# An mLSTM cell and a gated two-layer product: moving block sums, scalings and pair stores between engines and places

## The chip, the cores and the metric

The kernel runs on one core of one Trainium2 chip. The metric is the device time of one execution in microseconds (us), the median of several executions. One execution was taken by the hardware profiler; its own time is given beside its span below. The engines are named as the profile names them: PE is TensorE's matmul, PEld its weight load, DVE is VectorE, ACT is ScalarE, POOL is GpSimd, and SP is SyncE, whose queue (SPq) issues nearly all DMAs.

## The reference

The first half is a recurrent cell over 768 time steps, for 4 batches of 8 heads with head size 40. The second half is a two-layer product with a quick GELU between the layers, on the cell's output seen as 3072 tokens of 320 numbers. All is float32.

```python
for t in range(S):                                   # S = 768; B, H, D = 4, 8, 40
    m_new  = maximum(f_gate[t] + m, i_gate[t])
    f_stab = exp(f_gate[t] + m - m_new)
    i_stab = exp(i_gate[t] - m_new)
    C = f_stab * C + i_stab * outer(v[t], k[t])      # D x D for each head
    n = f_stab * n + i_stab * k[t]
    y[t] = sigmoid(o_gate[t]) * (C @ q[t]) / maximum(abs(n @ q[t]), 1)
x = y as (3072, 320)
h = x @ w_in                                         # w_in 320 x 2048
g = h * sigmoid(1.702 * h)
out = g @ w_out                                      # w_out 2048 x 320
```

## The kernel before, in words

**Rounds.** The 768 steps are cut into six windows of 128 (`w` = 0 to 5). A window of all four batches is 512 tokens. The loop at L807 runs one round per window: the *first product* of window w (`x @ w_in`), then the *second product* of window w (`g @ w_out`). The attention of window w+1 is laid between the parts of the second product, so that TensorE stays fed. Within each engine, instructions run in program order; the order is written out by hand and nothing is scheduled automatically.

**First product.** In round 0 it is done plainly (`up`, L545). In rounds 1 to 5 it is a Strassen-like scheme with seven products (`up_fast`, L608), in eight passes `j` = 0 to 7 of 256 hidden units each. A pass makes a tile `g` (128 partitions, 2 x 512): DVE adds parts at L658, L659 and L662, ACT copies at L655 and L666, GpSimd adds at L667 (for j below 6; DVE does it at L669 for the last two), and ACT applies GELU at L606 (`gelu_fast` of pass j-1 runs in pass j). In round 1, passes 0 to 3 also hold `weight_sums` (L687), one GpSimd operation of 128x1280 each. While a next window remains, DVE transposes its q and k in passes 1 to 6 (L353).

**Second product.** In round 0, `down` (L671) makes 16 blocks. In rounds 1 to 5, `down_fast` (L714) makes 14 blocks, seven for each pair `c` of batches (c = 0, 1); a block is one product of 16 TensorE matmul records, whose result DVE adds to an output tile (L730, L732). The scheme needs sums of hidden blocks. `a00`, `a10` and `a11` are `hidden(w, j, 0)`, `hidden(w, j, 1)` and `hidden(w, j + 4, 1)`, each 128x512. `hidden_sums` (L695) forms, for j = 0 to 3: s1 = a10 + a11 (L705), s2 = s1 - a00 (L706), and last, in place, a10 = a00 - a10 (L703). GpSimd does j = 0 and 1, after passes 6 and 7 of the first product (L845); DVE does j = 2 and 3 after the last pass (L849). `last_sums` (L708, DVE, L712) later turns s2 into a fourth sum. Block 2 reads s2, block 3 reads the changed a10, block 4 reads s1, block 6 reads the fourth sum.

**Attention of the next window.** `attention(w)` (L796) gives a table `at` of block numbers; after block i of the second product, all calls with that number run. For rounds 1 to 4 the numbers are 0, 0, 1, 3, 1, 4, 5, 6, 10, 12; for round 0 (argument w = 1) they are 0, 1, 3, 3, 5, 6, 8, 9, 13, 14. The calls are, in order:

- after block 0: `columns` (L320, ACT makes exponentials: L329 and then L333), `decay` for both pairs (L511, GpSimd, L516: state times a column that L333 made), and then `scale` for both pairs (L519, GpSimd, L523: v times a column that L329 made, giving `vw`).
- `weights` (L365, ACT L381 and GpSimd L385), `open_gates` (L335, ACT).
- `carry` (L525): TensorE multiplies k by `vw` into `p_c` (L533); DVE adds that to the decayed state (L542), with its own decay (L516, DVE) in between.
- `scores` (L388, TensorE L405, DVE L408), then `values` for each pair (L432): TensorE L449 and L457, DVE L463 and L464, then `outputs` (L410), which ends with two DVE operations at L424 that write the pair's rows `y`, one batch each.
- `seam_out` (L488): stores `y` to DRAM, two DMAs per batch (`x_row`, `x_rest`), called inside `outputs` after each batch. All are issued by SP.
- `seam_in` (L498): three SP loads bring the rows back in another layout (`q_sq<-x_row`, `q_sq<-x_rest` twice). `seam_turn` (L506): DVE transposes them into `xT` (L508), the input of the next first product.

In round 0, `input_sums` (L580, DVE L584 to L587, four operations of 128x512 per call) runs after blocks 11 and 12. `token_sums` (L589, DVE L595 to L600) opens each fast first product, and its sums feed the fifth product of pass 0.

Of the kernel before, what the change touches and what calls it, by code (L numbers as in the profile page):

```python
# [8 lines left out]
FP = mybir.dt.float32  # L9
# [3 lines left out]
OP = mybir.AluOpType  # L13
# [4 lines left out]
L = 128  # L18
# [8 lines left out]
def kernel(  # L27
# [12 lines left out]
    nc = tc.nc  # L40
# [22 lines left out]
    sp = ctx.enter_context(tc.tile_pool(name="sp", bufs=4))  # L63
    op = ctx.enter_context(tc.tile_pool(name="op", bufs=2))
    rows = ctx.enter_context(tc.tile_pool(name="rows", bufs=2, space=bass.MemoryType.DRAM))
# [4 lines left out]
    V, A, G, T = nc.vector, nc.scalar, nc.gpsimd, nc.tensor  # L70
# [38 lines left out]
    def load(w, what, bs=slice(0, B)):  # L109
        hs = slice(bs.start * H, bs.stop * H)  # L110
        for c in what:
            if c == "o" and w not in eo:
                eo[w] = ld.tile([L, BH, D], FP, tag="eo", bufs=1, name="eo")
            dst, src = {"k": (k_of(w), k), "q": (q_st, q), "v": (v_st, v), "o": (eo.get(w), o_gate)}[c]
            if w and c in "kv":
                for i, t, r in ((0, slice(0, L), slice(0, L)), (1, slice(0, HL), slice(HL, L)),
                                (1, slice(HL, L), slice(0, HL))):
                    x = src[:, :, w * L + t.start:w * L + t.stop, :].rearrange("b (p two) s d -> two s (b p) d", two=2)
                    nc.sync.dma_start(out=dst[r, i::2, 0:D], in_=x[i])  # L119
                continue  # L120
            nc.sync.dma_start(out=dst[:, hs, 0:D],
                              in_=src[bs, :, w * L:(w + 1) * L, :].rearrange("b h s d -> s (b h) d"))
# [97 lines left out]
    kT, qT, ys, xT, gs, o_ps, sums, vw, x_row = {}, {}, {}, {}, {}, {}, {}, {}, {}  # L220
# [189 lines left out]
    def outputs(w, hs, u):  # L410

        n = hs.stop - hs.start
        c, b = divmod(hs.start // H, 2)
        den = work.tile([L, n, 1], FP, tag="den", name="den")
        V.tensor_scalar(out=den, in0=u[:, :, D:D1], scalar1=-1.0, scalar2=1.0, op0=OP.mult, op1=OP.max)
        V.tensor_tensor(out=den, in0=u[:, :, D:D1], in1=den, op=OP.max)
        V.reciprocal(out=den, in_=den)
        z = eo[w][:, hs, :]
        V.scalar_tensor_tensor(out=z, in0=z, scalar=1.0, in1=u[:, :, 0:D], op0=OP.add, op1=OP.mult)
        if b == 0:  # L420
            ys[w, c] = work.tile([L, 2, DM + 64], FP, tag="y", name="y")
        for x in range(n // H):
            y, h = ys[w, c][:, b + x], slice(hs.start + x * H, hs.start + x * H + H)
            V.scalar_tensor_tensor(out=y[:, 0:DM].rearrange("p (h d) -> p h d", d=D), in0=eo[w][:, h, :], scalar=0.5,  # L424
                                   in1=den[:, x * H:(x + 1) * H].to_broadcast([L, H, D]), op0=OP.mult, op1=OP.mult)
            if w:
                seam_out(w, c, x)
        if w == 0:
            y = ys[w, c][:, b:b + n // H]
            G.tensor_copy(out=y[:, :, DM:DM + 64], in_=y[:, :, DM - 64:DM])  # L430
# [54 lines left out]
        at, m = (c * 768, 64) if n == 0 else (c * 768 + 512, 32)  # L485
        return q_sq[:, at:at + 8 * m].rearrange("r (b y) -> r b y", y=m)

    def seam_out(w, c, b):  # L488

        if b == 0:  # L490
            x_row[w, c] = (rows.tile([2, 4, L, 64], FP, name="x_row"), rows.tile([2, 2, L, 32], FP, name="x_rest"))
        y = ys[w, c][:, b, :]
        for x, at, m in ((x_row[w, c][0], 0, 64), (x_row[w, c][1], 256, 32)):
            g = x.shape[1]
            nc.sync.dma_start(out=x[b].rearrange("g t y -> t g y"),
                              in_=y[:, at:at + g * m].rearrange("t (g y) -> t g y", y=m))

    def seam_in(w, c):  # L498
        for n, gs_ in ((0, (0,)), (1, (0, 64))):
# [187 lines left out]
    def weight_sums(n):  # L687
        out, a, b = ((t1, w01, w00), (t2, w11, t1), (w01, w11, w01), (t4, w10, t2))[n]
        G.tensor_tensor(out=out, in0=a, in1=b, op=OP.subtract)

    def hidden(w, j, b):

        return gs[w, j].rearrange("p i (c two t) -> p i c two t", two=2, t=L)[:, :, :, b, :]

    def hidden_sums(w, j, late):  # L695
        if j % 2 == 0 and not late:
            for x in (1, 2):
                sums[w, x, j // 2] = sp.tile([128, 2, 2, 2, L], FP, tag="g", name="s")
        s1, s2 = (sums[w, x, j // 2][:, j % 2] for x in (1, 2))
        a00, a10, a11 = hidden(w, j, 0), hidden(w, j, 1), hidden(w, j + 4, 1)  # L700
        engine = G if j < 2 else V
        if late:
            engine.tensor_tensor(out=a10, in0=a00, in1=a10, op=OP.subtract)  # L703
        else:
            engine.tensor_tensor(out=s1, in0=a10, in1=a11, op=OP.add)  # L705
            engine.tensor_tensor(out=s2, in0=s1, in1=a00, op=OP.subtract)  # L706

    def last_sums(w, c, js):  # L708

# [38 lines left out]
    def run(calls):  # L748
        for f, *args in calls:
            f(*args)  # L750
# [39 lines left out]
    def weights_in(n):  # L790
        for p in beside[n][0]:
            convert(p)
        for p in beside[n][1]:
            fetch(p)

    def attention(w):  # L796
        at = (0, 1, 3, 3, 5, 6, 8, 9, 13, 14) if w == 1 else (0, 0, 1, 3, 1, 4, 5, 6, 10, 12)
        calls = [[(columns, w), (decay, w, 0, 0), (decay, w, 1, 0), (scale, w, 0), (scale, w, 1)],
                 [(weights, w, 0)], [(weights, w, 1)], [(carry, w, 0), (carry, w, 1)], [(open_gates, w)],
                 [(scores, w, 0), (scores, w, 1)], [(values, w, 0), (seam_in, w, 0)], [(values, w, 1), (seam_in, w, 1)],  # L800
                 [(seam_turn, w, 0)], [(seam_turn, w, 1)]]
        side = {}
        for i, c in zip(at, calls):
            side.setdefault(i, []).extend(c)
        return side

    for w in range(NW):  # L807
        more = w + 1 < NW
        if w == 0:
            for j in range(NF // 2):  # L810
                if j % 2 == 0:
                    weights_in(j // 2)
                    up(w, j)
                if j == 0:
                    load(1, "o")
                if j < B:
                    (carry if j % 2 else scale)(0, j // 2)
                if j == 3:
                    masks()
                    gates(1)  # L820
                if j == 4:
                    load(1, "v")
                    columns_in(1)
                    spread(1)
                if j >= B:
                    transposes(1, j - B)
        else:
            token_sums(w)
            if more:
                gates(w + 1)  # L830
                load(w + 1, "o")
            for j in range(NF // 2):
                up_fast(w, j)
                if w == 1 and j < 4:
                    weight_sums(j)
                if more and j == 2:
                    load(w + 1, "vk")
                    columns_in(w + 1)
                    spread(w + 1)
                if more and j:  # L840
                    for n in ((), (0, 2), (4,), (6, 1), (3,), (5, 7), ())[j - 1]:
                        block_transposes(w + 1, n)
                if more and j == 7:
                    columns_turn(w + 1)
                if j in (6, 7):  # L845
                    for late in (False, True):
                        hidden_sums(w, j - 6, late)
            gelu_fast(w, NF // 2 - 1)
            run([(hidden_sums, w, j, late) for late in (False, True) for j in (2, 3)])  # L849
        side = attention(w + 1) if more else {}  # L850
        if w == 0:
            columns_turn(1)

            blocks = [(lambda b=b, n=n: down(w, b, n)) for n0 in (0, 2) for b in range(B) for n in (n0, n0 + 1)]
        else:
            blocks = down_fast(w, 0) + down_fast(w, 1)
        for i, block in enumerate(blocks):
            if w == 0 and i < 6:
                weights_in(4 + i)
            if w + 2 < NW and i == (6 if w == 0 else 0):  # L860
                load_gates(w + 2)
            if w + 2 < NW and i == 13:
                load_squares(w + 2, "kq" if w else "k")
            if w == 0 and i == 15:
                load_squares(w + 2, "q")
            block()
            run(side.get(i, []))
            if w == 0 and i in (11, 12):
                input_sums(slice(0, 4) if i == 11 else slice(4, 8))


# [28 lines left out]
```

## Time and profile before

| what | value |
|---|---|
| times of three runs | 490.03, 488.68, 487.78 us; median 488.68 us |
| the profiled execution | 487.78 us, of which its span is 486.1 us |
| granted TensorE clock, mean | 0.998 |
| PE busy | 471.6 us (97%), 4926 instructions |
| DVE busy | 348.3 us (72%) |
| ACT busy | 189.7 us (39%) |
| POOL busy | 149.3 us (31%), 135 instructions |
| chain that ended last, by engine | PE 62%, POOL 10%, SPq 8%, DVE 6%, DMA 6% |
| POOL L705, L706, L703: one 128x512 operation | 1278, 1274, 1273 ns, ten of each |
| DVE L705, L706, L703: the same shapes | 670, 692, 901 ns, ten of each |
| POOL L516 (decay), L523 (scale) | 1155 ns, ten; 1398 ns, twelve |

A line of a timeline or group gives the start and the length in us, the engine, the code line, the operation, the tiles (written `out<-in`), their shapes and the count `xN` of instructions merged into the line. In square brackets stands how long the engine was idle before it and what ended that idleness. A list of waits reads: engine, tile and line that waited, `<-` what it waited for, then the total in us, how many times, and the longest. Matmuls are pipelined and the profile models their ends, so a line of TensorE may overlap the next one; distances between starts are the safer measure.

### The profile page before, as it was taken

To read this page: it belongs to the slowest core of one execution; us is meant where nothing else is said; L and a number is where in the kernel's file an instruction comes from. 1 tells how busy PE (TensorE), PEld (TensorE's weight loads), DVE (VectorE), ACT (ScalarE), POOL (GpSimd) and SP (SyncE) were. 2 spreads that over 40 slices of the span, in tenths; PEclk is the share of its full clock that TensorE was granted. 3 is DMA by queue.
4 is the path that set the end of the run, shared out by engine and by line. 5 is a ranking of instruction groups with operands and counts; after the bars stand their busy time and mean duration, and the time that the engine had idled before them with its cause. 6 is when DMAs were issued, how large, how long until landed. Compare 5 with 4: busy or idle time off the path is not lost.

```text
span 486.1 us, 12090 instructions
## 1 busy us (share of the span) xinstructions
PE 471.6 (97%) x4926; PEld 378.4 (78%) x4926; DVE 348.3 (72%) x691; ACT 189.7 (39%) x429; POOL 149.3 (31%) x135
## 2 busy tenths in 40 slices
PE   8999999999999999999999999999999999999995
PEld 5774446777668889767889877899877899877995
DVE  5675977988778975868985868985868965644711
ACT  4746558700453900354900254710254720254100
POOL 6020003400398700127620136630036630136100
PEclk9999999999999999999999999999999999999999
DMA  8999988005997014989304899604899504200000
GB/s 182 174 310 145 271 134 192 3 13 131 207 169 137 2 42 109 160 150 131 69 21 101 168 154 125 92 18 102 165 167 119 88 18 102 61 1 0 1 27 29
DMA packets 157352, 52.19 MB, mean 107 GB/s; under 512 B 127056, under 2 KB 154736, under 8 KB 157296
## 3 DMA queue, kind: packets, MB, share of 16 engines
q1 hardware_dynamic: 157296, 51.42, 56.9%
q8 instruction: 39, 0.64, 0.6%
q14 instruction: 17, 0.14, 0.1%
HBM read 43.86 MB, written 7.54 MB: 106 GB/s over the span
## 4 chain that ended last, share of the span: by engine, by line
PE 62%; POOL 10%; SPq 8%; DVE 6%; DMA 6%; issue 5%; ACT 2%; DVEq 0%; POOLq 0%
PE p_out L727 25%; PE p_h L625 15%; PE p_h L630 5%; PE p_h L555 4%; DMA wt<-m_row 3%; SPq L363 3%; PE p_o L449 2%; POOL vw L523 2%; SPq L119 2%; PE p_i L457 2%; POOL g L667 2%; SPq L311 2%; PE p_s L405 2%; PE p_out L676 1%; PE p_c L533 1%
## 5 line engine op out<-in xcount | busy, mean ns | idle before, releaser
L667 POOL TENSOR_TENSOR g<-g,parts 128x512 f32<-128x512 f32 x30 | 38.3, 1276 | 213.1 <-DVE parts L659 202.0
L655 ACT COPY parts<-p_h 128x256 f32<-128x256 f32 x40 | 15.0, 374 | 160.3 <-PE p_h L625 157.6
L727 PE MATMUL p_out<-w_out_sb,g 128*128 128x160 f32 x480 | 69.6, 301 | 0.1
L727 PEld LDWEIGHTS p_out<-w_out_sb,g 128*128 128x128 f32 x480 | 66.6, 190 | 1.1 <-issue 0.2
L625 PE MATMUL p_h<-xT,w_in_sb 128*128 128x256 f32 x240 | 66.9, 388 | 0.0
L606 ACT ACTIVATE g<-g 128x512 f32<-128x512 f32 x80 | 50.0, 631 | 36.2 <-DVE g L662 25.1
L625 PEld LDWEIGHTS p_h<-xT,w_in_sb 128*128 128x128 f32 x240 | 43.7, 190 | 20.2 <-issue 8.3
L732 DVE TENSOR_TENSOR o_sb<-o_sb,p_out 128x160 f32<-128x160 f32 x70 | 20.5, 315 | 41.5 <-PE p_out L727 20.8
L727 PE MATMUL p_out<-t_sb,s 128*128 128x160 f32 x320 | 47.1, 300 | 0.0
L658 DVE TENSOR_TENSOR t_x<-p_h,parts 128x256 f32<-128x256 f32 x40 | 16.7, 418 | 39.1 <-PE p_h L630 34.6
L727 PEld LDWEIGHTS p_out<-t_sb,s 128*128 128x128 f32 x320 | 44.4, 190 | 0.2
L625 PE MATMUL p_h<-t_x,s_in 128*128 128x256 f32 x160 | 41.1, 379 | 0.9 <-DVE t_x L595 0.9
L630 PE MATMUL p_h<-xT,w_in_x 64*128 64x512 f32 x160 | 39.7, 615 | 0.0
L381 ACT ACTIVATE wt<-wt,cols 128x64 f32<-128x64 f32 x160 | 38.8, 333 | 0.1
L676 PE MATMUL p_out<-w_out_sb,g 128*128 128x320 f32 x128 | 36.0, 436 | 0.7 <-DVE w_out_sb L234 0.7
L625 PEld LDWEIGHTS p_h<-t_x,s_in 128*128 128x128 f32 x160 | 30.3, 190 | 5.4 <-issue 1.3
L676 PEld LDWEIGHTS p_out<-w_out_sb,g 128*128 128x128 f32 x128 | 23.8, 190 | 10.6 <-DVE w_out_sb L234 1.2
L659 DVE TENSOR_TENSOR parts<-p_h,t_x 128x512 f32<-128x512 f32 x40 | 27.7, 692 | 3.5
L666 ACT COPY g<-p_h 128x512 f32<-128x512 f32 x30 | 17.4, 580 | 31.9 <-PE p_h L630 26.5
L555 PE MATMUL p_h<-xT,w_in_sb 128*128 128x512 f32 x64 | 29.5, 604 | 0.1
L516 POOL TENSOR_TENSOR state_mid<-state,cols 128x328 f32<-128x328 f32 x10 | 11.4, 1155 | 59.4 <-ACT cols L333 55.6
L662 DVE TENSOR_TENSOR g<-p_h,parts 128x512 f32<-128x512 f32 x40 | 27.7, 691 | 1.4
(185 smaller groups left out, 850.3 us busy)
## 6 DMA issues: line engine op xcount, KB each, us to landing
wt<-m_row SPq DMA_DIRECT2D x40, 128.0 KB, 3.7
k_sq<-in_k_dram SPq DMA_DIRECT2D x16, 320.0 KB, 6.2
q_sq<-in_q_dram SPq DMA_DIRECT2D x16, 320.0 KB, 10.1
out_dram<-o_sb SPq DMA_DIRECT2D x24, 160.0 KB
eo<-in_o_gate_dram SPq DMA_DIRECT2D x5, 640.0 KB, 8.9
bits<-in_moe_w_in_dram SPq DMA_DIRECT2D x6, 512.0 KB
x_row<-y SPq DMA_DIRECT2D x20, 128.0 KB, 2.4
q_sq<-x_row SPq DMA_DIRECT2D x10, 256.0 KB, 2.6
```

The costliest lines, as they stand in the source:

```text
L381: A.activation(out=x[:, h, :], in_=x[:, h, :], func=AF.Exp, scale=-1.0, bias=cols[w][:, c * PH + h:c * PH + h + 1])
L555: T.matmul(ph[j][i], w_in_sb[:, c, f * 128:(f + 1) * 128], x[:, c, :], start=(first and c == 0), stop=(not first and c == 1))
L606: A.activation(out=gs[w, j][:, i, :], in_=gs[w, j][:, i, :], func=AF.Gelu_apprx_sigmoid)
L625: T.matmul(out, a, x[n], start=start, stop=stop)
L630: T.matmul(row, w_in_x[r, j, :], rest_x[r, 2, :], start=not late, stop=late)
L659: V.tensor_tensor(out=y[:, half_w:3 * half_w].rearrange("p (a t) -> p a t", a=2), in0=flat[:, half_w:3 * half_w].rearrange("p (a t) -> p a ...
L662: V.tensor_tensor(out=g[:, 1, :], in0=row1, in1=y[:, half_w:3 * half_w], op=OP.add)
L666: A.copy(out=g[:, 0, :], in_=row0)
L667: G.tensor_tensor(out=g0, in0=g0, in1=u, op=OP.add)
L676: T.matmul(po, gs[w, f // 2][:, f % 2, b * L:(b + 1) * L], w_out_sb[:, f, :], start=(f == 0), stop=(f == NF - 1))
L727: T.matmul(po, a(f), b[:, f, :], start=(f == 0), stop=(f == NH - 1))
L732: V.tensor_tensor(out=dst, in0=x, in1=po, op=OP.add)
```

## The change

Four things change.

1. `hidden_sums` is split. `hidden_difference` does a10 = a00 - a10 first, for all four j, on GpSimd, after passes 2 to 5 of the first product, when the GELU of tile j is long done. The other sums are built on that difference d: s2 = a11 - d and then s1 = s2 + a00. GpSimd does them for j = 0, 1 after passes 6 and 7, DVE for j = 2, 3 after the last pass, with both s2 ahead of both s1.
2. In `attention`, the two `scale` calls stand ahead of the two `decay` calls.
3. `seam_out` is a call of its own for a whole pair instead of a call per batch inside `outputs`. It issues both batches' `x_row` stores and then both `x_rest` stores. For pair 1 ScalarE issues them instead of SP. In rounds 1 to 4, pair 0's stores and loads follow block 6 instead of block 5.
4. In round 0, `seam_turn` of pair 0 follows block 12 instead of 13, and the second `input_sums` follows block 13 instead of 12.

```diff
     def outputs(w, hs, u):
...
-            if w:
-                seam_out(w, c, x)
...
-    def seam_out(w, c, b):
+    def seam_out(w, c):
...
-            nc.sync.dma_start(out=x[b].rearrange("g t y -> t g y"),
-                              in_=y[:, at:at + g * m].rearrange("t (g y) -> t g y", y=m))
+            for b in range(2):
+                (nc.scalar if c else nc.sync).dma_start(
+                    out=x[b].rearrange("g t y -> t g y"),
+                    in_=ys[w, c][:, b, at:at + g * m].rearrange("t (g y) -> t g y", y=m))
...
-    def hidden_sums(w, j, late):
...
-        engine = G if j < 2 else V
-        if late:
-            engine.tensor_tensor(out=a10, in0=a00, in1=a10, op=OP.subtract)
-        else:
-            engine.tensor_tensor(out=s1, in0=a10, in1=a11, op=OP.add)
-            engine.tensor_tensor(out=s2, in0=s1, in1=a00, op=OP.subtract)
+    def hidden_difference(w, j):
+
+        a00, a10 = hidden(w, j, 0), hidden(w, j, 1)
+        G.tensor_tensor(out=a10, in0=a00, in1=a10, op=OP.subtract)
+
+    def hidden_sums(w, js, engine):
+        for j in js:
...
+            d, a11 = hidden(w, j, 1), hidden(w, j + 4, 1)
+            engine.tensor_tensor(out=sums[w, 2, j // 2][:, j % 2], in0=a11, in1=d, op=OP.subtract)
+        for j in js:
+            s1, s2 = (sums[w, x, j // 2][:, j % 2] for x in (1, 2))
+            engine.tensor_tensor(out=s1, in0=s2, in1=hidden(w, j, 0), op=OP.add)
...
-        at = (0, 1, 3, 3, 5, 6, 8, 9, 13, 14) if w == 1 else (0, 0, 1, 3, 1, 4, 5, 6, 10, 12)
-        calls = [[(columns, w), (decay, w, 0, 0), (decay, w, 1, 0), (scale, w, 0), (scale, w, 1)],
+        at = (0, 1, 3, 3, 5, 6, 8, 8, 9, 12, 14) if w == 1 else (0, 0, 1, 3, 1, 4, 5, 6, 6, 10, 12)
+        calls = [[(columns, w), (scale, w, 0), (scale, w, 1), (decay, w, 0, 0), (decay, w, 1, 0)],
...
-                 [(scores, w, 0), (scores, w, 1)], [(values, w, 0), (seam_in, w, 0)], [(values, w, 1), (seam_in, w, 1)],
-                 [(seam_turn, w, 0)], [(seam_turn, w, 1)]]
+                 [(scores, w, 0), (scores, w, 1)], [(values, w, 0)], [(seam_out, w, 0), (seam_in, w, 0)],
+                 [(values, w, 1), (seam_out, w, 1), (seam_in, w, 1)], [(seam_turn, w, 0)], [(seam_turn, w, 1)]]
...
-                if j in (6, 7):
-                    for late in (False, True):
-                        hidden_sums(w, j - 6, late)
+                if 2 <= j < 6:
+                    hidden_difference(w, j - 2)
+                if j >= 6:
+                    hidden_sums(w, (j - 6,), G)
             gelu_fast(w, NF // 2 - 1)
-            run([(hidden_sums, w, j, late) for late in (False, True) for j in (2, 3)])
+            hidden_sums(w, (2, 3), V)
...
-            if w == 0 and i in (11, 12):
+            if w == 0 and i in (11, 13):
                 input_sums(slice(0, 4) if i == 11 else slice(4, 8))
```

More of the change, by code (lines that the diff above doesn't have):

```diff
@@ L486, in x_square @@
         return q_sq[:, at:at + 8 * m].rearrange("r (b y) -> r b y", y=m)
-    def seam_out(w, c, b):
-        if b == 0:
-            x_row[w, c] = (rows.tile([2, 4, L, 64], FP, name="x_row"), rows.tile([2, 2, L, 32], FP, name="x_rest"))
-        y = ys[w, c][:, b, :]
+    def seam_out(w, c):
+        x_row[w, c] = (rows.tile([2, 4, L, 64], FP, name="x_row"), rows.tile([2, 2, L, 32], FP, name="x_rest"))
         for x, at, m in ((x_row[w, c][0], 0, 64), (x_row[w, c][1], 256, 32)):
             g = x.shape[1]
-            nc.sync.dma_start(out=x[b].rearrange("g t y -> t g y"),
-                              in_=y[:, at:at + g * m].rearrange("t (g y) -> t g y", y=m))
+            for b in range(2):
+                (nc.scalar if c else nc.sync).dma_start(
+                    out=x[b].rearrange("g t y -> t g y"),
+                    in_=ys[w, c][:, b, at:at + g * m].rearrange("t (g y) -> t g y", y=m))
     def seam_in(w, c):
@@ L693, in hidden @@
         return gs[w, j].rearrange("p i (c two t) -> p i c two t", two=2, t=L)[:, :, :, b, :]
-    def hidden_sums(w, j, late):
[L696 to L700, printed above, removed]
-        engine = G if j < 2 else V
-        if late:
-            engine.tensor_tensor(out=a10, in0=a00, in1=a10, op=OP.subtract)
-        else:
-            engine.tensor_tensor(out=s1, in0=a10, in1=a11, op=OP.add)
-            engine.tensor_tensor(out=s2, in0=s1, in1=a00, op=OP.subtract)
+    def hidden_difference(w, j):
[3 more added lines that the diff above has]
+        for j in js:
+            if j % 2 == 0:
+                for x in (1, 2):
+                    sums[w, x, j // 2] = sp.tile([128, 2, 2, 2, L], FP, tag="g", name="s")
+            d, a11 = hidden(w, j, 1), hidden(w, j + 4, 1)
[3 more added lines that the diff above has]
+            engine.tensor_tensor(out=s1, in0=s2, in1=hidden(w, j, 0), op=OP.add)
     def last_sums(w, c, js):
```

## The prediction, made blind

> **What bounds the kernel now.** I read the busy times first, then the list of waits, then TensorE's timeline round by round, and last the timelines of whoever it waits for. TensorE is busy 97% of the 486.1 us span, so only its idle time can go.
>
> ```profile
> PE 471.6 (97%) x4926; PEld 378.4 (78%) x4926; DVE 348.3 (72%) x691; ACT 189.7 (39%) x429; POOL 149.3 (31%) x135
> ```
>
> ```profile
> PE p_c L533 <- POOL vw L523: 3.5, 8, 0.6
> PE p_i L457 <- issue: 1.7, 2, 1.0
> ...
> PE p_h L625 <- DVE t_x L595: 0.9, 1, 0.9
> ```
>
> Three kinds matter: eight waits of the carry for scaled values, one at the start of round 1, and two in which it waited for nothing visible. The first kind, in round 2, on TensorE, on GpSimd and on ScalarE:
>
> ```profile
> 236.06 2.34 PE L727 MATMUL p_out<-w_out_sb,g 128*128 128x160 f32 x16
> 238.97 1.14 PE L533 MATMUL p_c<-vw,k_st 64*64 64x41 f32 x64 [0.57 <-POOL vw L523]
> 240.40 1.14 PE L533 MATMUL p_c<-vw,k_st 64*64 64x41 f32 x64 [0.28 <-POOL vw L523]
> 241.47 2.44 PE L727 MATMUL p_out<-t_sb,s 128*128 128x160 f32 x16
> 243.84 2.10 PE L405 MATMUL p_s<-qT,kT 40*64 40x64 f32 x128
> ```
>
> ```profile
> 235.25 2.42 POOL L516 TENSOR_TENSOR state_mid<-state,cols 128x328 f32<-128x328 f32 x2 [3.74 <-ACT cols L333]
> 237.63 2.71 POOL L523 TENSOR_TENSOR vw<-v_st,cols 128x656 f32<-128x656 f32 x2
> ```
>
> ```profile
> 234.50 0.26 ACT L329 ACTIVATE cols<-cols 128x64 f32<-128x64 f32 x1
> 234.66 0.51 ACT L333 ACTIVATE cols<-raw 64x32 f32<-64x32 f32 x2
> ```
>
> GpSimd, idle until 235.25, does two decays first, and TensorE waits for each scaling in turn. The start of round 1, on TensorE and on DVE:
>
> ```profile
> 120.86 1.03 PE L625 MATMUL p_h<-xT,w_in_sb 128*128 128x256 f32 x4
> ...
> 123.42 1.10 PE L625 MATMUL p_h<-t_x,s_in 128*128 128x256 f32 x4 [0.90 <-DVE t_x L595]
> ...
> 127.44 0.70 PE L625 MATMUL p_h<-xT,w_in_sb 128*128 128x256 f32 x2
> ```
>
> ```profile
> 121.06 0.71 DVE L508 STREAM_TRANSPOSE xT<-q_sq 128x512 f32<-128x512 f32 x1 [1.72 <-DMA q_sq<-x_row]
> ```
>
> Here pair 1's rows come back late, so L508 is late, so the sums of L595 are late.
>
> **What the Trainium skill says.** "Perfetto Trace Analysis" (Identifying the Most-Contended Engine) warns that matmul busy time is no good measure of headroom. The trace agrees in small: the carry's second wait shows 0.28 us idle, but 0.43 is lost by distances of starts. So I measure stalls by starts. "SBUF — State Buffer" (Who interferes with whom) says that a DVE instruction with two SBUF inputs contends with a GpSimd one that reads SBUF, and one with at most one SBUF input, outside the 2-port modes, doesn't. The trace agrees: a pair of L712 (two SBUF inputs) takes 0.75 us with GpSimd idle (457.19) and 2.76 beside the scalings (237.87); a transpose L353 takes 1.14 beside a GpSimd addition (219.34), 1.10 without (220.30). "DMA: Bandwidth & Descriptors" (Issuing engines are not separate DMA queues) says that a second issuing engine saves only the sequencer's time. Here just that is late: in round 0 SP issued pair 1's first store at 113.73, though DVE had finished both rows at 112.0 (L424, 111.12 + 0.89).
>
> **Part 1, scalings ahead of decays.** From a product to small matmuls the starts lie 243.84 - 241.47 = 2.37 apart. Unhindered, the carry would start at 236.06 + 2.37 = 238.43; it starts at 238.97, 0.54 late. One carry takes 1.0 (in round 0 both took 2.01 with no wait, 85.86 to 87.87), so the second would start at 239.97, but does at 240.40, 0.43 late. Rounds 1, 3 and 4 give 0.54 to 0.55 for the first (164.63 for 164.09, 313.20 for 312.66, 386.61 for 386.06) and about the same second. Sum 4 x 0.97 = 3.9 us. Afterwards a scaling waits for L329 alone, which ends at 234.76: at 1.36 us each the scalings end at 236.1 and 237.5, at the trace's longest (1.73) at 236.5 and 238.2. TensorE needs them at 238.43 and 239.43, so all 3.9 goes with 1.2 to spare. The decays now run from 237.5 to 239.9 (1.18 each); queued behind them are the four masks L385, which began at 240.30 before, so nothing there is later. DVE's L542 wants decay and carry, and the carry itself ends only at 239.4. Next late at the carry would be k_st, issued by 223.9 and landing some 6.0 us later, at 230: no danger. Round 0's carry did not wait, so nothing is won there.
>
> **Part 2, the sums.** DVE loses two L703 a round (1.83 us at 235.25). GpSimd gains two operations, 2 x 1.27, and all four differences move into passes 2 to 5, where it idles 2.0 to 3.6 us ahead of each L667 in rounds 2 to 5. They fit, and the sums behind them, four operations instead of six, end near 230.2 instead of 231.5. DVE, with both s2 first, has them by 234.0; block 2 needs the third at 233.89 + 1.09 = 234.98. Block 3 loses a wait that did not stall. Value zero, hidden by TensorE's own products. But DVE must now keep up with a TensorE 1 us earlier: L408 of pair 0 ended 247.5 and was needed at 248.24. The 1.83 us saved covers that; without it 0.3 us a round would come back.
> Round 1 is the tight place, as weight_sums fill GpSimd there:
>
> ```profile
> 141.84 1.28 POOL L667 TENSOR_TENSOR g<-g,parts 128x512 f32<-128x512 f32 x1
> 143.06 2.92 POOL L689 TENSOR_TENSOR t_sb<-w_out_sb,t_sb 128x1280 f32<-128x1280 f32 x1
> 145.94 1.28 POOL L667 TENSOR_TENSOR g<-g,parts 128x512 f32<-128x512 f32 x1
> 148.43 1.28 POOL L667 TENSOR_TENSOR g<-g,parts 128x512 f32<-128x512 f32 x1 [1.21 <-ACT g L666]
> ```
>
> Three differences push pass 4's L667 to end near 149.65 (from 147.2). ScalarE's GELU waits for it, and queued behind that is the copy L666 of pass 5, then done at about 150.8 (from 148.4). TensorE rewrites that buffer in pass 7 at 150.96. Cost 0, at most 0.4 us.
>
> **Part 3, stores and transposes.** Round 0: ScalarE, idle from 94.7 to 121.5, issues pair 1's four stores from 112.05, some 0.45 us each by SP's rows; nothing waits behind them. The second x_row goes out near 112.5 instead of 114.82, so SP's loads start about 2.3 us earlier than 118.23, though still after pair 0's (until 113.05). The last rows land by about 120, not 121.9; L508 runs by 120.7, DVE copies the last block by 121.4, and L595 ends near 121.85. TensorE wants it at 122.2. Pass 0 took 127.44 - 120.86 = 6.58 us against 276.00 - 270.97 = 5.03 in round 3: 1.55 lost, of which I take 1.5; if the loads land 1 us later than I think, 0.6.
> Rounds 1 to 4: pair 0's stores wait behind block 6's output store (ready 0.4 us after them, issue 0.6), about 1 us later, but its loads were issued by 260.45 for a transpose at 266.14. SP no longer holds block 6's store from 254.7 to 260.54, so DVE's wait for an output buffer (4.74 us at 264.77) goes. Both off the path: zero.
> The two issue waits (0.96 at 181.20, 0.78 at 255.47) fall just after SP's x_row stores; moving those may end them or not. Between a gain of 1.8 and a loss of 1.0 (as much again in a round spared so far), I take zero.
>
> **Sum.** 3.9 + 1.5 = 5.4 us. The profiled execution took 487.78, 1.7 more than its span; it would take 482.4. The median of the three runs lies 0.9 above that execution, so I forecast 483.3.
>
> **Rivals.**
> *A, the issue waits go too:* 483.3 - 1.8 = 481.5. For it: both followed the stores by half a microsecond. Against: rounds 3 and 4 issued the same stores at the same place without one.
> *B, only the scalings pay:* the loads of round 0 still arrive after 121.5, because their 2.4 to 3.3 us to landing don't shrink. 488.7 - 3.9 = 484.8.
> *C, the carry doesn't move as said:* something I can't see, a buffer of p_c or a later scaling, is late next; only round 1's start pays, 488.7 - 1.5 = 487.2. Against it: every other input of the carry is 1 us early or more.
> *D, slower:* the differences block DVE in passes 2 to 5. Two passes of round 3 hold 1.38 us of DVE idle time (at 291.68), so it decides from 0.69 us per difference; at a full 1.27 each, two passes lose 2 x 1.27 - 1.38 = 1.16. Twice in each of four rounds: 9.3 us. 488.7 + 9.3 - 5.4 = 492.6. Against it: the L353 pair of the SBUF rule above, and DVE's additions there read PSUM and keep 0.69 us beside L667.
>
> **How the numbers follow.** Forecast 0.52 (own range 482.0 to 484.6: parts 1 and 3 within their bounds), A 0.16, B 0.14, C 0.11, D 0.07. The measurement can tell about 0.5% from no change, 2.4 us. Faster by more holds forecast, A and B: 0.82; within it C, 0.11; slower D, 0.07. The range from 481.0 to 487.0 takes in A and B, and leaves out most of C, and D.
>
> **What would show it.** Right: no p_c wait on vw, starts 2.37 and 1.0 apart at the carry; rounds 2 to 4 about 1 us shorter each; L508 of pair 1 before 121, no wait on L595; L703 inside passes 2 to 5 on GpSimd with L353 still 1.1. Wrong: a TensorE wait on ACT in pass 7 of round 1, L353 or L659 longer, or a new wait at p_o or p_s for L408 or L542.

## The result and the profile after

The changed kernel took 481.97 us (median of six runs, 481.72 to 483.82), against 489.36 us (six runs, 487.78 to 491.04) for the kernel before, measured beside it. The ratio is 0.9854, with a 95% interval from 0.9824 to 0.9885. The forecast was 483.3, the range 481.0 to 487.0. The time is right; the experiments show that a good part of the reason is not.

The profiled execution is the longest of the six, 483.82 us with a span of 481.8. TensorE's granted clock was 0.73 in the mean there between 178.9 and 185.3 us, and 32 matmuls of round 1 (starts from 179.14 to 185.27) took 6.13 us instead of the 4.46 that they take in other rounds (398.12 to 402.58); these 1.67 us are not the change's. The other five executions have spans of 479.5 to 480.0.

The busy times, from the page after:

```profile
PE 471.4 (98%) x4926; PEld 379.7 (79%) x4926; DVE 336.8 (70%) x681; ACT 189.4 (39%) x429; POOL 158.0 (33%) x145
```

TensorE works as long as before in a shorter span. GpSimd has ten operations and 8.7 us more, DVE ten operations and 11.5 us fewer. TensorE's waits after (total, times, longest):

```profile
PE p_i L455 <- issue: 2.1, 2, 1.3
PE p_idle L189 <- DVE one L197: 1.1, 1, 1.1
PE p_out L674 <- DVE w_out_sb L234: 0.7, 1, 0.7
PE p_s L394 <- DVE wt L396: 0.5, 1, 0.5
PE p_t L345 <- DMA q_sq<-in_q_dram: 0.4, 1, 0.4
...
```

The eight waits of the carry for `vw` and the wait for `t_x` are gone; the two in which it waited for nothing visible have stayed. The 0.4 us for a load of q stand at 6.0 us, ahead of all that was changed, and had no like in the list of before. Round 2's carry, on TensorE and then on GpSimd (start, duration):

```profile
235.44 2.34 PE L728 MATMUL p_out<-w_out_sb,g 128*128 128x160 f32 x16
237.71 2.08 PE L531 MATMUL p_c<-vw,k_st 64*64 64x41 f32 x128
239.72 2.44 PE L728 MATMUL p_out<-t_sb,s 128*128 128x160 f32 x16
```

```profile
234.21 2.75 POOL L521 TENSOR_TENSOR vw<-v_st,cols 128x656 f32<-128x656 f32 x2 [4.56 <-ACT cols L329]
236.92 1.79 POOL L514 TENSOR_TENSOR state_mid<-state,cols 128x328 f32<-128x328 f32 x2
```

Product, both pairs' carry and next product start 2.27 and 2.01 us apart. They were 2.91 and 2.50 before, so 0.64 and 0.49, together 1.13 us a round, are saved. The start of round 1, on DVE:

```profile
119.56 1.03 DVE L506 STREAM_TRANSPOSE xT<-q_sq 128x512 f32<-128x512 f32 x2
120.93 0.49 DVE L678 COPY o_sb<-p_out 128x320 f32<-128x320 f32 x1 [0.34 <-PE p_out L674]
121.34 0.42 DVE L593 TENSOR_TENSOR t_x<-xT 128x256 f32<-128x256 f32 x1
```

Pair 1's transposes no longer wait for a DMA and end before 121. Pass 0 takes 5.19 us (120.73 to 125.92) instead of 6.58.

Where the time went, by the starts of the first products: rounds 2, 3 and 4 take 73.10, 72.17 and 72.04 us; they took 74.20, 73.42 and 73.17, so 1.10, 1.25 and 1.13 are saved. Round 1 takes 75.40 instead of 75.91. Without the 1.67 of the clock it saves 2.18: 1.39 in pass 0, 1.14 at the carry, less 0.32 by which its wait for nothing visible is longer. The rest is unchanged: from the start of the last second product to the end of DVE's last operation it was 30.95 and is 30.95 us.

So far all looks as predicted. What the changed kernel can't show is which part paid.

### The profile page after: what moved, and what is told of

Read it like the earlier page. It is cut to its first block, busy times and chain, and to the rows that moved or that the text cites. A ratio compares the mean times of both kernels' runs of the same rounds, so it can differ in the third digit from the quotient of the medians.

```text
span 481.8 us, 12086 instructions
## 1 busy us (share of the span) xinstructions
PE 471.4 (98%) x4926; PEld 379.7 (79%) x4926; DVE 336.8 (70%) x681; ACT 189.4 (39%) x429; POOL 158.0 (33%) x145
## 4 chain that ended last, share of the span: by engine, by line
PE 91%; DVE 3%; SPq 2%; POOL 1%; issue 1%; DMA 1%; ACT 0%; POOLq 0%; DVEq 0%
PE p_out L728 33%; PE p_h L623 26%; PE p_h L628 8%; PE p_out L674 7%; PE p_h L553 5%; PE p_c L531 3%; PE p_o L447 2%; PE p_s L405 2%; PE p_i L455 2%; PE p_h L559 1%; PE p_o L437 1%; DMA wt<-m_row 1%; SPq L363 1%; PE p_t L345 1%; SPq L119 0%
## 5 line engine op out<-in xcount | busy, mean ns | idle before, releaser
L728 PE MATMUL p_out<-w_out_sb,g 128*128 128x160 f32 x480 | 71.3, 306 | 0.0
L728 PEld LDWEIGHTS p_out<-w_out_sb,g 128*128 128x128 f32 x480 | 68.2, 194 | 1.1
L733 DVE TENSOR_TENSOR o_sb<-o_sb,p_out 128x160 f32<-128x160 f32 x70 | 21.5, 319 | 45.8 <-PE p_out L728 45.4
L521 POOL TENSOR_TENSOR vw<-v_st,cols 128x656 f32<-128x656 f32 x12 | 16.6, 1402 | 59.8 <-ACT cols L329 59.8
L674 PEld LDWEIGHTS p_out<-w_out_sb,g 128*128 128x128 f32 x128 | 23.8, 190 | 10.6 <-DVE w_out_sb L234 1.2
L657 DVE TENSOR_TENSOR parts<-p_h,t_x 128x512 f32<-128x512 f32 x40 | 27.7, 692 | 3.5
```

The source lines that it names most:

```text
L657: V.tensor_tensor(out=y[:, half_w:3 * half_w].rearrange("p (a t) -> p a t", a=2), in0=flat[:, half_w:3 * half_w].rearrange("p (a t) -> p a ...
L674: T.matmul(po, gs[w, f // 2][:, f % 2, b * L:(b + 1) * L], w_out_sb[:, f, :], start=(f == 0), stop=(f == NF - 1))
L728: T.matmul(po, a(f), b[:, f, :], start=(f == 0), stop=(f == NH - 1))
L733: V.tensor_tensor(out=dst, in0=x, in1=po, op=OP.add)
```

## The experiments

The theory on trial first was the prediction's own: part 1 (scalings first) is worth 3.9 us, part 3 (stores) 1.5, part 2 (sums) nothing. The rival, that only the parts together do it, had no mechanism yet. All times are medians; ratios are to the kernel before, measured beside each.

### One part at a time

**Scalings first alone**, on the kernel before:

```diff
-        calls = [[(columns, w), (decay, w, 0, 0), (decay, w, 1, 0), (scale, w, 0), (scale, w, 1)],
+        calls = [[(columns, w), (scale, w, 0), (scale, w, 1), (decay, w, 0, 0), (decay, w, 1, 0)],
```

> The kernel before with one edit: the two scalings stand ahead of the two decays. Theory (the carry's stall on the scaled values is the main part): 2.7 to 3.9 us faster than before, no wait of L533 on vw in rounds 1 to 4; if DVE, still with its L703, cannot follow, up to 0.3 us a round shows up as a new TensorE wait at p_o or p_s. Rival (the saved DVE time of the moved sums is what pays): within 1 us of before.

Measured: 488.99 against 488.19 us, ratio 1.0013 (1.0 to 1.0026). No gain at all. The carry's wait is gone, but another has its place. Its list of waits, then DVE and GpSimd in round 2:

```profile
PE p_out L727 <- DVE g L703: 3.5, 4, 0.9
```

```profile
234.64 3.47 DVE L703 TENSOR_TENSOR g<-g 128x512 f32<-128x512 f32 x2
```

```profile
234.22 3.34 POOL L523 TENSOR_TENSOR vw<-v_st,cols 128x656 f32<-128x656 f32 x2 [3.34 <-ACT cols L329]
```

DVE's two differences take 3.47 us instead of 1.83, since GpSimd now runs the scalings beside them, and block 3, which reads them, waits 0.88 us per round. The scalings are held up too: 3.34 instead of 2.71. By starts the carry of round 2 takes 2.00 us instead of 2.50, and block 3 ahead of it 3.46 instead of 2.91.

**Sums alone**, on the kernel before (`hidden_difference` and the new `hidden_sums`, as in the diff of the change):

> The kernel before with only the block sums moved and rebuilt (four differences on GpSimd in passes 2 to 5). Theory: within 0.5 us of before, the stall of the carry unchanged at 0.5 to 0.6 us on its first matmul, L353 still 1.1 us in passes 2 to 5. Rival (the sums pay): 2 us or more faster. Rival (GpSimd blocks DVE): slower, L353 above 1.5 us.

Measured: 484.55 us, ratio 0.9919 (0.9905 to 0.9934), about 4 us faster by the ratio. The part priced at zero is the largest. GpSimd in its round 2:

```profile
233.89 1.43 POOL L516 TENSOR_TENSOR state_mid<-state,cols 128x328 f32<-128x328 f32 x2 [4.96 <-DMA wt<-m_row]
235.28 2.90 POOL L523 TENSOR_TENSOR vw<-v_st,cols 128x656 f32<-128x656 f32 x2
```

The decays still come first, but a pair takes 1.43 us, not 2.42: DVE ended its sums at 233.83 and is out of the way. From block 3 to the carry and on it is 2.27 and 2.33 us (starts at 234.70, 236.97, 239.30), against 2.91 and 2.50 before. Of the 1.13 lost per round 0.33 is left, with the order untouched; the 0.80 won is 3.2 us in four rounds.

**Stores alone**, on the kernel before (`seam_out`, the table `at` and the place of the input sums):

> The kernel before with only the stores, their places, ScalarE as issuer for pair 1, and round 0's transposes and input sums moved. Theory: 1.5 us faster than before, all of it at the start of round 1 (pass 0 there 5.0 us instead of 6.6), the carry's stall in rounds 1 to 4 as before. Rival (stores matter in every round): 3 us or more.

Measured: 487.19 us, ratio 0.9978 (0.9965 to 0.999), about 1 us faster. `t_x` is not waited for, and the carry's wait is as before:

```profile
PE p_c L531 <- POOL vw L521: 3.5, 8, 0.6
PE p_i L455 <- issue: 2.3, 2, 1.3
```

**Everything but the scalings**, the changed kernel with the decays first again:

> The changed kernel with the decays ahead of the scalings again. Theory: 3.9 us slower than the changed kernel, about 1.5 to 2 us faster than before; L533 waits on vw eight times again. Rival (the sums pay): within 1 us of the changed kernel.

Measured: 482.53 us, ratio 0.989 (0.9866 to 0.9915), 0.56 more than the changed kernel and not 3.9. Its carry in round 2:

```profile
235.74 2.41 PE L531 MATMUL p_c<-vw,k_st 64*64 64x41 f32 x128
238.07 2.44 PE L728 MATMUL p_out<-t_sb,s 128*128 128x160 f32 x16
```

2.33 us from start to start, where the changed kernel has 2.01: again 0.33 lost per round, 1.3 in four rounds. The times bound it loosely: 0.56 between the medians, 1.8 between the ratios. (In the profiled executions the waits for nothing visible are 0.6 us in all here and 2.1 in the changed kernel; they may cover part of the stall in the medians.)

So the theory had fallen. The new one: **the decays were slow because DVE ran beside them**. Two operations that each take two values from SBUF, one on DVE and one on GpSimd, hold each other up. Before, the decays and DVE's differences L703 both began at 235.25. DVE's line of then, and the shortest, middle and longest time (ns) of one decay (the shortest is of round 0, where no L703 runs):

```profile
235.25 1.83 DVE L703 TENSOR_TENSOR g<-g 128x512 f32<-128x512 f32 x2
```

```profile
L516 POOL TENSOR_TENSOR state_mid<-state,cols x10: 736/1182/1283, 80.2 to 384.1; 128x328 f32<-128x328 f32 x10
```

The sums cure this by taking two operations off DVE; the order on GpSimd alone only chooses which pair of operations meets.

### The contention by itself

**Only the two differences of DVE left out**, on the kernel before:

```diff
-            run([(hidden_sums, w, j, late) for late in (False, True) for j in (2, 3)])
+            run([(hidden_sums, w, j, False) for j in (2, 3)])
```

> The kernel before, in which DVE leaves out the two differences L703 of hidden blocks 2 and 3 that it did last (block 3 of each second product then multiplies values that half lack their difference); everything else, the decays first too, is as before. Theory (the decays were slow because they ran beside these two operations on DVE; each took 1.2 us instead of 0.7): the pair of decays takes 1.43 instead of 2.42 us, the scalings come 1.0 earlier, the carry loses 0.33 a round instead of 0.97, and the time falls by 2.6 us or more, to 485.6 or less; as far as 484.5 if all of what the sums alone won comes from this. Rival 1 (the gain of the sums alone came from the new form, in which s2 is ready first, or from GpSimd's free time): no gain, 488.2. Rival 2 (it came from issue waits that happened to shrink from 1.7 to 0.9): 488.2, with a shorter stall at the carry and longer issue waits.

Measured: 483.99 us, ratio 0.991 (0.9891 to 0.9929). GpSimd and TensorE in round 2:

```profile
233.89 1.43 POOL L516 TENSOR_TENSOR state_mid<-state,cols 128x328 f32<-128x328 f32 x2 [3.77 <-ACT cols L333]
```

```profile
236.97 2.41 PE L533 MATMUL p_c<-vw,k_st 64*64 64x41 f32 x128
239.31 2.44 PE L727 MATMUL p_out<-t_sb,s 128*128 128x160 f32 x16
```

The old form of the sums, the old order and no work more for GpSimd: the same 1.43, the same 2.34, and as much gain as the sums alone. The new form of the sums (rival 1) is not needed for it. Issue waits (rival 2) are 0.9 us here and 1.7 before: 0.8 of the 4.4 us between the medians, while the carry's 0.80 a round makes 3.2.

**Two additions put back on DVE**, on the changed kernel with the decays first (482.53):

```diff
             hidden_sums(w, (2, 3), V)
+            spare = work.tile([128, 2, 2, L], FP, tag="y", name="spare")
+            for j in (2, 3):
+                V.tensor_tensor(out=spare, in0=hidden(w, j, 0), in1=hidden(w, j + 4, 1), op=OP.add)
```

> The kernel after with the decays first again (the run of that name took 482.53), and on DVE, behind the four sums of hidden blocks 2 and 3, two additions more of two values in SBUF (128x512, 0.65 us each), whose result nobody reads. They fall beside GpSimd's decays and scalings. Theory (DVE and GpSimd hold each other up): decays and scalings together take 1.2 to 1.3 us longer than 4.3, the carry's wait for vw comes back at 1.0 to 1.5 us a round in four rounds, and the time is 4 to 6 us longer, 486.5 to 488.5. Rival (only DVE's own lateness counts): decays and scalings keep 1.43 and 2.9, no wait for vw, and as much longer as the same kernel with the transposition: 0 to 1 us.

**One transposition instead of them:**

```diff
             hidden_sums(w, (2, 3), V)
+            spare = work.tile([128, 512], FP, tag="y", name="spare")
+            for j in (3,):
+                V.transpose(out=spare, in_=gs[w, j].rearrange("p a b -> p (a b)")[:, 0:512])
```

> As the kernel with the two extra additions, but with one transposition on DVE instead of them (128x512, one value in SBUF, 1.1 us), whose result nobody reads. Theory (only operations with two values in SBUF hold GpSimd up): decays and scalings keep 1.43 and 2.9 us a pair, no new wait at the carry, and 482.5 to 483.5. Rival (any work of DVE beside GpSimd holds it up, or DVE's lateness itself costs): the decays and scalings take 1 us longer, 485 to 487.

Measured: with the additions 485.64 us, ratio 0.9946 (0.9929 to 0.9963); with the transposition 482.40, ratio 0.9875 (0.9856 to 0.9895), no more than without. In the kernel with the additions, DVE, GpSimd and TensorE's wait:

```profile
234.09 1.83 DVE L854 TENSOR_TENSOR spare<-g 128x512 f32<-128x512 f32 x2
```

```profile
234.24 2.27 POOL L514 TENSOR_TENSOR state_mid<-state,cols 128x328 f32<-128x328 f32 x2 [4.97 <-DMA wt<-m_row]
```

```profile
PE p_c L531 <- POOL vw L521: 3.0, 8, 0.6
```

In the kernel with the transposition, DVE and GpSimd:

```profile
232.25 0.70 DVE L854 STREAM_TRANSPOSE spare<-g 128x512 f32<-128x512 f32 x1
```

```profile
232.40 1.43 POOL L514 TENSOR_TENSOR state_mid<-state,cols 128x328 f32<-128x328 f32 x2 [4.96 <-DMA wt<-m_row]
```

Two additions bring back all three signs of before: 1.83 on DVE, 2.27 instead of 1.43 on GpSimd, eight waits of the carry. The transposition leaves the decays at 1.43. Its list has three short waits of the carry for `vw`, 0.5 us in all, which were not expected; by starts the carry loses 0.03 us a round more than without it. DVE's copies and additions of a product from TensorE (L731, L733, 0.32 us each), which have at most one value in SBUF, lie beside these decays too. Two reservations: the transposition took 0.70 us, not the 1.1 expected, so it met the first decay for 0.55 us only; and the additions cost 3.1 us, less than the 4 to 6 expected. The scalings behind them took 2.71 us, no longer than without them (2.90), and by starts the carry lost 1.00 us a round instead of 0.33.

**Scalings first and stores, without the sums:**

> The kernel after with the sums of before: scalings ahead of decays and the new stores, without the third difference on GpSimd. The prediction's own steps give 483.3 for it (the sums were worth nothing). The theory that the sums carry the gain: the scalings run beside DVE's L703, block 3 waits for L703 some 0.9 us a round as in the scalings alone, and only the 1.0 us of the stores is left: 487 to 488.5.

Measured: 487.35 us, ratio 0.9974 (0.9961 to 0.9986), what the stores alone give. Its list of waits:

```profile
PE p_out L725 <- DVE g L701: 3.5, 4, 0.9
```

The prediction's steps give 483.3 for this kernel. They are 4 us off.

### What ScalarE's issuing is worth

```diff
-                (nc.scalar if c else nc.sync).dma_start(
+                nc.sync.dma_start(
```

> The kernel after with one edit: SP, not ScalarE, issues the stores of pair 1 too. It tells what ScalarE's issuing is worth beside the later place of the stores. Theory (the 1.4 us at the start of round 1 come from ScalarE's earlier issue): SP issues pair 1's stores behind pair 0's loads again, L506 of pair 1 is late, TensorE waits for L593 at the start of round 1 some 0.9 us, and the time is 1.0 to 1.5 us longer than after, 483 to 483.5. Rival (the regrouping of the stores does it): 482.

Measured: 482.51 us, ratio 0.9863 (0.9839 to 0.9887), 0.54 more than the changed kernel and half of what was expected. The intervals of the two kernels overlap, so the trace has to decide. TensorE's wait at the start of round 1:

```profile
PE p_h L623 <- DVE t_x L593: 0.5, 1, 0.5
```

0.47 us instead of 0.90 before. SP issues both `x_row` stores back to back now, from 112.97, so the load of these rows goes out at 115.90 instead of 118.23 and the large transposition runs at 119.54; only the rows of `x_rest`, loaded at 118.17, are late. About half of the wait goes by ScalarE's issuing. The other half goes by the grouping, or by the moved transposes and input sums of round 0, which were not tried alone.

### The waits for nothing visible

In TensorE's timelines of both kernels and of all nine experiments so far these two waits stand at the same place: behind 56 or 57 of the 64 matmul records of pair 1's `p_i` in round 1 and behind 62 or 63 in round 2 (a record or so can be missing), whatever the stores do. Only their length differs, 0.25 to 1.3 us. The kernel with the sums alone has a third one, which the expectations below overlook: 0.57 us in round 3, behind the fourth record of the product after `p_i`. In its list of waits:

```profile
PE p_out L730 <- issue: 0.6, 1, 0.6
```

Counted in TensorE's matmul records, it comes 886 behind the one of round 2, as that comes 886 behind the one of round 1. In the changed kernel the one of round 2 began at 252.9, before its `x_row` stores were issued at 253.55. So three kernels moved the place: idle matmuls at the start, `keep_busy`, were put as fewer or more instructions with about the same streaming time.

```diff
-    keep_busy(8)
+    keep_busy_f(2)
...
-    keep_busy(4)
+    keep_busy_f(1)
```

`keep_busy_f` is the same in fp32, 512 columns each.

> The kernel after with 9 matmuls fewer on TensorE before round 0's products: twelve idle bf16 ones are put as three fp32 ones of half the width of output, with the same streaming time. It shifts the place of every later instruction in TensorE's program by 9 matmuls and changes nothing else. The two waits for nothing visible (2.1 us, at the 57th matmul of 64 of p_i in round 1 and at the last in round 2; the same two places in every kernel so far, whatever the stores do) are open. Theory (they belong to a place in the instruction stream): both move by 9 matmuls and so out of p_i into the products behind it; in rounds 3 and 4, where no wait is seen, the same count already puts the place there. Then up to 2 us less than after: 480 to 481.5. Rival 1 (they belong to transfers or to p_i itself): same two places in p_i, 482. Rival 2: they follow the count but stay as long or longer in the products: 482 to 483.

```diff
-    keep_busy(8)
+    for _ in range(17):
+        T.matmul(p_idle[:, 0:240], idle, idle[:, 0:120].unsqueeze(1).to_broadcast([128, 2, 120]), start=True, stop=True)
```

> The kernel after with 9 matmuls more at the start: eight idle ones of 512 columns are put as seventeen of 240, the same streaming time. Theory of the place in the instruction stream: the waits of rounds 1 and 2 move 9 matmuls forward in p_i (to about the 48th and the 55th of 64), and round 3, whose place then comes to about the 62nd, gets one too: three waits, up to 1 us longer than after, 482 to 483.5. Rival (transfers, or p_i itself): two waits at the same places, 482.

Measured: with fewer 480.75 us, ratio 0.9827 (0.9803 to 0.9851); with more 482.78, ratio 0.9865 (0.9844 to 0.9886). TensorE's rows with such a wait, all of over 0.15 us, in the kernel with fewer and in the one with more:

```profile
178.63 0.25 PE L461 MATMUL p_i<-state_mid,qT 40*64 40x41 f32 x1 [0.60 <-issue]
```

```profile
174.61 2.20 PE L729 MATMUL p_out<-w_out_sb,s 128*128 128x160 f32 x15 [0.99 <-issue]
...
251.63 0.25 PE L456 MATMUL p_i<-state_mid,qT 40*64 40x41 f32 x1 [0.89 <-issue]
...
324.80 0.25 PE L456 MATMUL p_i<-state,qT 40*64 40x41 f32 x1 [0.70 <-issue]
```

The trace counts an fp32 matmul as two records, so "9 fewer" was 6 fewer. Counted in records ahead of the wait: with 6 fewer, round 1's has gone from 57 to 63, and round 2's out of `p_i`. With 9 more, round 2's has come from 63 to 54, round 3 has one, behind 60, and round 1's, which would come to 48, stands behind the first record of a product instead, 127 records earlier (15 of the product, 64 of `p_o`, 48 of `p_i`). Three waits, as expected, one of them 127 records from where it was expected.

**Eleven fewer**, that kernel with one idle matmul instead of two in five calls:

```diff
-            keep_busy(2)
+            keep_busy(1)
...
-    keep_busy(2)
+    keep_busy(1)
```

> The kernel with the three fp32 idle matmuls in place of twelve, and of its other idle ones five fewer. The trace counts each fp32 matmul twice, so that kernel had moved the places by 6, not by 9: the wait of round 1 went from the 57th matmul of p_i to the 63rd, and that of round 2 from the 63rd into the products, where none is seen. Here the shift is 11 in all. Theory of the place in the instruction stream: round 1's place comes to about the 68th, four matmuls into the products, where rounds 2 and 3 of earlier kernels had no wait; no wait for nothing visible on p_i or p_out is left, and the time falls by 0.6 us more, to 480.2. Rival: one such wait a kernel remains wherever the place is, 480.75 or more; or the colder clock at the start costs what the wait gave.

Measured: 479.73 us (479.60 to 479.84), ratio 0.9819 (0.9799 to 0.984). Its list of waits has no wait for nothing visible on a matmul any more, and the granted clock was 1.00 from 0 to 125 us, as in the kernel with fewer. Rounds 1 to 4 now take 72.32, 72.04, 72.04 and 72.03 us. All its runs lie 1.88 us or more below the shortest of the changed kernel, though not in one session, and the intervals of the two ratios overlap. Against the kernel with fewer it won 1.0 us between the medians and 0.4 between the ratios, where 0.6 was expected.

## Why the prediction was right in its sum and wrong in its parts

- **The stall of the carry, 3.9 us: right in place, somewhat low in size, wrong in cause.** By starts 1.13 to 1.14 us per round went, 4.5 in four. The prediction took 2.37 us from a product to the unhindered carry, a distance read at other matmuls; 2.27 is what the changed kernel needs. The failed step is in part 2: "Value zero, hidden by TensorE's own products", with "Block 3 loses a wait that did not stall". The sums won about 4 us alone; the scalings alone won nothing (1.0013). The failed claim in part 1 is "all 3.9 goes with 1.2 to spare": without the sums, what the carry no longer loses, block 3 loses, which then waits 0.88 us per round. What rival C had feared was so without the sums: something not seen was late next (C's time was 487.2, scalings and stores together took 487.35).
- **Where the reading went wrong.** The prediction quoted the Trainium skill, "SBUF — State Buffer" (Who interferes with whom), on two values from SBUF, and used it for L712 and for GpSimd's new differences. It did not lay it over the one place where DVE's L703 and the decays both start at 235.25. The means in the page of before showed it: L703 at 901 ns where the same shape took 670 in L705. And the decays' 2.42 us was taken as their own length, while it is 1.43 undisturbed. The page calls the port pair that DVE and GpSimd share an exclusive lock. The trace agrees nearly: 1.83 us of DVE and 2.42 of GpSimd lie in one stretch of 2.42, where the undisturbed pairs (1.35 for two additions of that shape, 1.43) add up to 2.78. One by one, the first L703 kept 0.69, as in round 5 where no decay runs; then the first decay took 1.28 and the second L703 1.22, against 0.74 and 0.68 undisturbed, so each was held up in turn.
- **The order on GpSimd** is worth what is left when DVE is out of the way: 0.33 us a round in the starts, 1.3 in four rounds (0.56 between the medians, 1.8 between the ratios).
- **Part 3, 1.5 us: right.** Pass 0 fell by 1.39, and the stores alone gave about 1 us. About half of it comes without ScalarE, which the prediction didn't count apart. Pair 1's transposes ended at 120.59, so rival B fell too.
- **The other zeros held.** GpSimd's last addition of pass 4 in round 1 ended at 148.17; TensorE runs 1.5 us earlier there than before, so against it this is as late as the 149.65 that was forecast, and TensorE did not wait. DVE's additions beside the differences kept 692 ns (L657; L659 before), its transposes 1.10 to 1.16 us (1.08 to 1.17 before): rival D fell. No wait at `p_o` for L408 or at `p_s` came up.
- **Issue waits at zero: right for the change, by luck.** They don't belong to the stores (rival A), but to a place in TensorE's stream that the change left as it was.
- **1.3 us more than forecast.** The carry gave 0.6 to 0.7 us more than counted. Another 0.9 is what the forecast added because the median of the three runs before lay that much above the profiled one; of the six runs after, five lie within 0.4 us, and no such distance shows. Against that stand 0.35 us more of waits for nothing visible in the profiled execution and 0.3 more outside the span; the rest are terms of 0.1 to 0.2 us.

What stays open: why the waits for nothing visible differ in length, 0.25 to 1.3 us at nearly the same place, and what TensorE waits for there. That a place in the stream sets them was shown by moving it; what happens at that place was not.

## What to carry to other kernels

When a step on GpSimd is late, compare its duration, and that of what DVE does at that moment, with the same shapes elsewhere: a mean longer than that of its twins can be a meeting of two engines, and reordering one of them may only move it. Price each part of a change in the presence and in the absence of the others, as two parts can share one stall. In a stretch of very short matmuls, a wait for nothing visible that keeps its place in every version can be tried by a few instructions more or fewer ahead of it.

## What the runs showed of the hardware

- Pairs of operations with two SBUF values each, one engine beside the other: DVE's 128x512 pair 1.35 us alone, 1.83 beside the decays, 3.47 beside the scalings. GpSimd's pair of decays took 1.43 with no such operation of DVE beside it and 2.27 to 2.42 with one; its pair of scalings 2.53 without (at 33.12), 2.71 to 2.90 beside DVE's fourth sums (L712), and 3.34 beside L703.
- A DVE transposition of 128x512 took 0.70 us with rows left in place, and 1.1 in L353's rearranged form.
- TensorE can pause 0.25 to 1.3 us for nothing visible in stretches of short matmuls. The place went with the count of instructions when it was moved by 6 and by 9 records, and a second such place was found 127 records away. The kernel with eleven records fewer at the start took about 2 us less in 480.
